# Up projection of five blocks by twenty block products per four row tiles, with chains begun from copies in PSUM

## The chip, the cores and the metric

The kernel runs on one core of a Trainium2 chip. The core has five engines with a queue each, and every engine works through its queue strictly in order: TensorE (PE, matrix products into PSUM), VectorE (DVE), ScalarE (ACT), GpSimd (POOL) and SyncE (SP, which here issues the DMAs). They wait for one another by semaphores. The metric is the device time of one execution in microseconds; of several executions the median is given.

## The reference

Two layers follow one another. The first is a linear attention with a state that decays per channel (4 sequences, 8 heads, 768 steps, 48 channels a head):

```python
for t in range(S):
    cur = einsum('bhd,bhe->bhde', u[None] * k[t], v[t])
    y[t] = einsum('bhd,bhde->bhe', r[t], state + cur)
    state = w[t][:, :, :, None] * state + einsum('bhd,bhe->bhde', k[t], v[t])
```

Its output, as 3072 tokens of 384 channels, goes through two projections with a gate in between:

```python
h = x @ w_in                        # (3072, 384) @ (384, 2048)
g = h * clip(h + 3.0, 0.0, 6.0) / 6.0
return g @ w_out                    # (3072, 2048) @ (2048, 384)
```

All of it is in fp32.

## The kernel before, in words

The 3072 tokens are 24 chunks of 128 (`L`), and four chunks make a block (`BC`), so there are six blocks, 0 to 5. The steps of attention of a chunk are two scans over its decays on VectorE (`back_scan` L372, `fore_scan` L381), scaling of r and k by them (`make_k`, `make_r`), a diagonal by eight small ScalarE operations (`diagonal` L431), scores and states on PE (`score` L440, `read_state` L514, `read_values` L523, `write` L536), and copies that put the result, transposed, into the block's `xT` (`leave` L606). Some channels take a way by DMA (`last_pair`, the steps `move`).

A block then is projected up and down. With 128 rows to a tile, the up projection has 16 row tiles of output (2048), 3 tiles of contraction (384, `NCC`) and 4 chunks as columns. The output stands transposed in two tiles `g0` and `g1`, one for each half of the block's 512 columns (`HB` = 256). The down projection takes one half at a time.

Block 0 is projected as written: three matmuls for each row tile and column group (`up` L639), then `clip` (L629) and `gate` (L650), and the first two chunks' `down` (L658) plain too. Blocks 1 to 5 use a fast block algorithm in which sums of blocks go into fewer products. Before the change it is a two-by-two scheme of Strassen's kind: for each of the eight pairs of row tiles (`q`), seven products over the first two tiles of contraction, with the third tile's four plain matmuls put into them, so 11 matmuls of 256 columns (`up_product` L740) in place of 12. The sums of weights are made once (`sum_in` L700), those of x once a block (`sum_x` L722, steps `tx`). Three banks of PSUM, `bankA`, `bankB` and `bankC`, hold a pair's sums. An intermediate value that two outputs need is read out of the bank and the next product added to the same bank after that. `up_read` does these reads, seven a pair: four copies on ScalarE (L749) and three adds on VectorE (L751). One of the copies (`u`) lies between products 6 and 7 of one bank. Each pair's outputs are then clipped (L629, ScalarE) and gated (L759, VectorE), 512 columns at a time.

The down projection of the half block, `p`, is likewise seven products of eight matmuls with 192 columns (`down_product` L791), in two parts of four matmuls, with sums on VectorE (`sum_g` L776, `sum_out` L712) and reads (`down_read` L804 and L806).

No engine's order is written out by hand. `Plan` holds each step with its engine, an assumed duration, what it comes after, a key (a due time in us, counted from the start of block 0's projection) and the rings of buffers that it holds until other steps have ended. Its `order` picks the step that could start earliest by the assumed durations, and of those that could start then the one with the smallest key; the steps are issued in that order, which fixes each queue. The assumed durations have no part in the running kernel apart from that order. `BASE` gives the blocks' due times, `START`, `CONV` and `UP` those of the first chunks, of the conversion of the weights from 64-bit floats (L340 to L359) and of block 0's up projection. Until the first up matmul (`up0.0.0`) the plan fills gaps on PE with products of an identity (`spin`, L1130).

The program for `sum` steps marks `port=True` for operations[...] and keeps them apart from each other.

The functions that the diff touches:

Of the kernel before, what the change touches and what calls it, by code (L numbers as in the profile page):

```python
# [27 lines left out]
LAG = 6.1  # L28
AHEAD = -3.5
LEAD = 2.5  # L30
BEHIND = (-1, -1, -1, 0, 6, 7)
BY_PE = 9
OWN = 0.07
SOLO = (0, 2, 3, 4, 5)
EARLY = 7
START = (-118.3, -135.2, -24.4, -60.3, -5.9, 13.2)
CONV = (-100.6, 7.2)
UP = (-68.7, 1.2, -9.3, 6.3)
SUMS = (52.1, 1.4)
LEAST = 2.0 ** -60  # L40

# [41 lines left out]
class Plan:  # L83
# [5 lines left out]
    HOP = 0.2  # L89
# [20 lines left out]
    def order(self):  # L110
# [13 lines left out]
        while open_:  # L124
            best = {}
            for n in open_:
# [4 lines left out]
                for a in after:  # L131
                    if steps[a][0] != engine:
                        t = max(t, end[a] + self.HOP)
                for r, _ in hold:
                    over = len(held[r]) - self.rings[r]
                    if over >= 0:
                        ends = sorted(max(end[a] + (self.HOP if steps[a][0] != engine else 0.0) for a in frees)
# [50 lines left out]
def fast_path(tc, feat, tok, wflat, ub, ug, moe_w_in, moe_w_out, out, flag, n_chunks):  # L188
# [21 lines left out]
    with ExitStack() as ctx:  # L210
# [34 lines left out]
        def constants():  # L245
# [16 lines left out]

            new_x(0)
# [99 lines left out]
        for r, k in (("E", 1), ("K", 2), ("W", 2), ("rk", 1), ("dg", 2), ("A", 2), ("kn", 1), ("S", 2), ("x", 2), ("kvs", 1), ("y", 1),  # L363
                     ("ps", 1), ("bankA", 2), ("bankB", 1), ("bankC", 2), ("clip", 2), ("g0", 1), ("g1", 1), ("o", 2),
# [68 lines left out]
        def score(i):  # L433
            d = st[i]
            d["a_ps"] = [pp.tile([128, P, HL], F32, name="bankB"), pp.tile([128, P, HL], F32, name="bankC", bufs=2)]
# [195 lines left out]
        def bank(name):  # L631
            return pp.tile([128, 512], F32, name=name, bufs=1 if name == "bankB" else 2)


        def up(f, c0, c1):
            b = blocks[0]
            h_ps = b["h", f, c0] = bank("bankA" if f % 2 else "bankC")
# [15 lines left out]
        def down(c, f0, f1):  # L653
            b = blocks[0]
            if f0 == 0:
                b["o", c] = bank("bankA")
# [23 lines left out]
        a_sums = {}  # L680
        b_sums = {}

        def a_slot(s, q):
            at = s * HF + q
            return a_sums[at // 6][:, at % 6 * 128:(at % 6 + 1) * 128]

        def sum_in(s, q):

            at = (s - 1 if s < 3 else 2) * HF + q
            if s != 3 and at // 6 not in a_sums:  # L690
                name = ("top", "more")[at // 6 % 2]
                a_sums[at // 6] = wk.tile([128, 6 * 128], F32, name=name)
            (a11, a21), (a12, a22) = ([w_in[:, q:q + 2, j, y, :] for y in range(2)] for j in range(2))
            def sums(k):
                at = k * HF + q
                return a_sums[at // 6][:, at % 6 * 128:(at % 6 + 2) * 128].rearrange("p (q j) -> p q j", q=2)
# [97 lines left out]
        def down_read(bk, p, what):  # L794
            b = blocks[bk]
            h = DM // 2
            if what == "s1":
                b["y", p] = wk.tile([L, 2, DM], F32, name="o")
# [671 lines left out]
```

## Time and profile before

| | us |
|---|---|
| median of 3 runs | 573.64 |
| the three runs | 573.64, 581.17, 572.21 |
| span of the profiled execution, first to last instruction | 570.5 |
| what lies between that span and the median; and the lowest run | 3.1; 1.7 |
| first matmul of block 0's up projection | 32.3 |
| first up matmul of blocks 1 to 5 | 151.8, 234.6, 320.6, 405.1, 489.0 |
| last matmul's end | 565.2 |

The profile gives no device time for the profiled execution itself, only its span; so the span stands beside the runs. The stretch before 32.3 us is attention for the first chunks with identity products in the gaps; then come block 0 (to 151.8) and five blocks. Attention for a later block is spread between the products of the one before. In the profile's groups "L740" is the line of the kernel, "bankA<-xT,w_in" the tile written and those read, "128x256" partitions by elements. An fp32 matmul of this kernel leaves two records, so 88 matmuls of an up projection are 176.

### The profile page before, as it was taken

To read this page: it belongs to the slowest core of one execution; us is meant where nothing else is said; L and a number is where in the kernel's file an instruction comes from. 1 tells how busy PE (TensorE), PEld (TensorE's weight loads), DVE (VectorE), ACT (ScalarE), POOL (GpSimd) and SP (SyncE) were. 2 spreads that over 40 slices of the span, in tenths; PEclk is the share of its full clock that TensorE was granted. 3 is DMA by queue.
4 is the path that set the end of the run, shared out by engine and by line. 5 is a ranking of instruction groups with operands and counts; after the bars stand their busy time and mean duration, and the time that the engine had idled before them with its cause. 6 is when DMAs were issued, how large, how long until landed. Compare 5 with 4: busy or idle time off the path is not lost.

```text
span 570.5 us, 13575 instructions
## 1 busy us (share of the span) xinstructions
PE 558.8 (98%) x5636; PEld 501.8 (88%) x5636; DVE 405.2 (71%) x713; ACT 273.5 (48%) x724; POOL 100.3 (18%) x111
## 2 busy tenths in 40 slices
PE   8999899999999999999999999999999999999996
PEld 8898587689888999988999988999988999988996
DVE  7989989988687858767879767879656625255350
ACT  4778664642565633276633366633266611355100
POOL 2000000245513321223123133123122000000000
PEclk9989899999999999999999999999999999999999
DMA  8977822531613236830368360366100001000001
GB/s 279 310 237 223 275 66 63 158 111 42 182 56 90 87 124 204 241 100 9 125 206 274 98 167 7 128 199 225 41 16 2 9 1 36 29 1 1 1 15 47
DMA packets 23078, 63.98 MB, mean 112 GB/s; under 512 B 3120, under 2 KB 10352, under 8 KB 23008
## 3 DMA queue, kind: packets, MB, share of 16 engines
q1 hardware_dynamic: 22880, 63.02, 36.0%
q8 instruction: 46, 0.75, 0.6%
q14 instruction: 24, 0.20, 0.1%
q10 hardware_dynamic: 128, 0.00, 0.0%
HBM read 57.31 MB, written 4.72 MB: 109 GB/s over the span
## 4 chain that ended last, share of the span: by engine, by line
PE 94%; DVE 2%; DMA 1%; ACT 1%; issue 1%; SPq 0%; DVEq 0%; ACTq 0%
PE bankA L791 20%; PE bankA L740 18%; PE bankC L791 10%; PE bankC L740 9%; PE bankB L740 6%; PE bankB L791 5%; PE bankC L639 3%; PE bankA L639 3%; PE bankA L658 3%; PE y_ps L514 3%; PE y_ps L523 2%; PE y_ps L536 2%; PE ps L456 2%; PE bankB L440 2%; DMA feat_in<-in_feat_dram 1%; PE bankA L1130 1%
## 5 line engine op out<-in xcount | busy, mean ns | idle before, releaser
L749 ACT COPY g<-bankA 128x256 f32<-128x256 f32 x120 | 44.3, 371 | 58.7 <-PE bankA L740 56.6
L791 PE MATMUL bankA<-w_out,g 128*128 128x192 f32 x352 | 63.9, 328 | 0.0
L629 ACT ACTIVATE clip<-g,three 128x512 f32<-128x512 f32 x80 | 57.9, 723 | 7.9 <-DVE g L751 7.2
L740 PE MATMUL bankA<-xT,w_in 128*128 128x256 f32 x240 | 60.2, 383 | 0.0
L791 PEld LDWEIGHTS bankA<-w_out,g 128*128 128x128 f32 x352 | 57.9, 190 | 0.9
L759 DVE SCALAR_TENSOR_TENSOR g<-clip,g 128x512 f32<-128x512 f32 x80 | 56.4, 707 | 2.8 <-ACT clip L629 2.6
L804 ACT ACTIVATE o<-bankA 128x192 f32<-128x192 f32 x33 | 10.9, 330 | 88.8 <-PE bankA L791 88.8
L740 PEld LDWEIGHTS bankA<-xT,w_in 128*128 128x128 f32 x240 | 44.8, 190 | 6.0
L431 ACT ACTIVATE A<-eyes,dg 128x64 f32<-128x64 f32 x192 | 49.2, 336 | 0.4
L606 ACT COPY xT<-y_ps 48x256 f32<-48x256 f32 x80 | 29.3, 366 | 37.3 <-PE y_ps L523 36.4
L392 POOL TENSOR_TENSOR K<-feat_in,E 112x512 f32<-112x512 f32 x17 | 21.5, 1266 | 136.6 <-PE bankC L440 121.6
L740 PE MATMUL bankB<-xT,w_in 128*128 128x256 f32 x160 | 41.1, 379 | 0.0
L751 DVE TENSOR_TENSOR g<-bankB,g 128x256 f32<-128x256 f32 x40 | 16.9, 423 | 32.4 <-PE bankB L740 30.7
L396 POOL TENSOR_TENSOR W<-feat_in,W 112x512 f32<-112x512 f32 x17 | 23.1, 1356 | 87.2 <-DVE W L381 87.2
L751 DVE TENSOR_TENSOR g<-bankC,g 128x256 f32<-128x256 f32 x40 | 16.8, 421 | 28.3 <-PE bankC L740 28.2
L740 PEld LDWEIGHTS bankB<-xT,w_in 128*128 128x128 f32 x160 | 30.4, 190 | 4.1
L381 DVE TENSOR_TENSOR_SCAN W<-feat_in,start 112x520 f32<-112x520 f32 x24 | 30.6, 1274 | 3.1 <-PE y_ps L514 3.0
L372 DVE TENSOR_TENSOR_SCAN E<-feat_in,back 112x520 f32<-112x520 f32 x24 | 30.0, 1250 | 2.5 <-DMA feat_in<-in_feat_dram 2.4
L791 PE MATMUL bankA<-bits,g 128*128 128x192 f32 x176 | 30.3, 328 | 0.4 <-DVE o L806 0.4
L791 PE MATMUL bankB<-w_out,g 128*128 128x192 f32 x176 | 30.4, 326 | 0.0
L791 PEld LDWEIGHTS bankA<-bits,g 128*128 128x128 f32 x176 | 28.8, 190 | 0.9 <-DVE o L806 0.7
L791 PEld LDWEIGHTS bankB<-w_out,g 128*128 128x128 f32 x176 | 28.9, 190 | 0.0
(277 smaller groups left out, 1213.8 us busy)
## 6 DMA issues: line engine op xcount, KB each, us to landing
feat_in<-in_feat_dram SPq DMA_DIRECT2D x23, 675.9 KB, 5.6
bits<-in_moe_w_in_dram SPq DMA_DIRECT2D x8, 768.0 KB, 9.6
bits<-in_moe_w_out_dram SPq DMA_DIRECT2D x8, 768.0 KB, 4.7
feat_in<-in_moe_w_in_dram SPq DMA_DIRECT2D x8, 768.0 KB, 4.3
feat_in<-in_moe_w_out_dram SPq DMA_DIRECT2D x8, 768.0 KB, 4.2
rk_in<-in_tok_dram SPq DMA_DIRECT2D x15, 384.0 KB, 5.9
v_in<-in_tok_dram SPq DMA_DIRECT2D x24, 192.0 KB, 4.0
out_dram<-o SPq DMA_DIRECT2D x24, 192.0 KB, 2.1
```

The costliest lines, as they stand in the source:

```text
L372: nc.vector.tensor_tensor_scan(out=E_[:, ::-1], data0=d["w"][:, :0:-1], data1=back.rearrange("q p t -> q (p t)")[:, ::-1], initial=0.0, op ...
L381: nc.vector.tensor_tensor_scan(out=W_, data0=d["w"][:, :-1], data1=starts[i % 2].rearrange("q p t -> q (p t)"), initial=0.0, op0=ALU.mult, ...
L396: early(i).tensor_mul(d["R"], d["r"], d["R"])
L431: nc.scalar.activation(out=d["A"][:, h, :], in_=eyes, func=ACT.Copy, scale=d["dg"][:, h])
L606: nc.scalar.copy(out=blocks[bk]["xT"][g * GP:g * GP + D, :, at:at + HL], in_=st[i]["y_ps"][(g ^ a) * GP:(g ^ a) * GP + D, a, :, :])
L629: nc.scalar.activation(out=c[:, :m], in_=src, func=ACT.Relu, bias=three, scale=1.0)
L639: nc.tensor.matmul(h_ps[:, :(c1 - c0) * L], lhsT=w_in[:, f // 2, j, f % 2, :], rhs=b["xT"][:, j, c0 * L:c1 * L], start=(j == 0), stop=(j = ...
L740: nc.tensor.matmul(b["p", q, to][:, :HB], lhsT=w, rhs=rhs, start=(n == 0 and k in (1, 2, 5)), stop=(n == len(terms) - 1 and k in (2, 3, 4) ...
L749: nc.scalar.copy(out=to, in_=src)
L751: nc.vector.tensor_add(to, src, to)
L759: nc.vector.scalar_tensor_tensor(out=g, in0=b["r", q, p], scalar=6.0, in1=g, op0=ALU.min, op1=ALU.mult)
L791: nc.tensor.matmul(b["d", p, to][:, :h], lhsT=a, rhs=w(), start=(f == 0 and k in (1, 2, 5)), stop=(f == HF - 1 and k in (2, 3, 4)), skip_g ...
```

## The change

The up projection of blocks 1 to 5 takes four row tiles together: four row tiles by three tiles of contraction by two column halves are 24 plain block products, and a scheme of 20 is used. There are two passes a block (`d`), each over two such groups (`z`), whose 256-column results lie side by side in one bank of 512. A product is then two matmuls, a pass 20 products, a block 80 matmuls. Instead of seven reads of 256 columns for each of eight pairs there are 19 of 512 columns for each of two passes: 8 on ScalarE and 11 on VectorE.

The sums of weights become 21 (`W_SUMS`), 128x512 each, once; nine of them write over `w_in` itself, after the last up product of block 0. The sums of x become 11 a block (`X_SUMS`), 128x256 each, in four steps.

Products are chained: `CHAINS` lists, for each bank, products (numbers) and reads (names) in the order that they must have. Some chains do not begin with an empty bank: ScalarE copies another chain's bank into the one bank `bankS` (reads `a4` and `a14`), and the next product adds to that. The down projection uses the same means: its read `s1` becomes a copy of bank A into `bankS`, product 2 adds to it and ScalarE reads `c11` out in one go; products 2 and 5 change places. The four bank names become one ring of four, `bank`, besides `bankS`. One product of zeros writes `bankS` at the start.

`WHEN` gives the due position of each of the 20 products in a pass; the last, 22, falls into the next pass. All due times are new, and so are the planner's assumed durations, the wait between engines among them (`HOP`). A parameter of the program for DMA scratch memory is set to 4096.

```diff
-LAG = 6.1
-AHEAD = -3.5
-LEAD = 2.5
+LAG = 8.196
+AHEAD = -4.96
+LEAD = -2.25
-START = (-118.3, -135.2, -24.4, -60.3, -5.9, 13.2)
-CONV = (-100.6, 7.2)
-UP = (-68.7, 1.2, -9.3, 6.3)
-SUMS = (52.1, 1.4)
+START = (-127.21, -154.12, -36.12, -115.85, 30.64, 32.42)
+CONV = (-75.91, 4.42)
+UP = (-75.43, 3.62, -8.89, 6.07)
+SUMS = (104.45, 0.18, 45.29)
+W_PLACE = ("e1", "e3", "e2", "w2", "w3", "w6", "e7", "w9", "e6", "w5", "w4", "w8", "e4", "w1", "w11", "e5", "w0", "w10", "e0", "w7")
+X_PLACE = ("w2", "e2", "e8", "e3", "w0", "e4", "w4", "w3", "w0", "e0", "e5", "w1", "w1", "w5", "e9", "w2", "e7", "w3", "e1", "e6")
+X_PARTS = (0, 4, 7, 9, 11)
+CHAINS = ((14, "a0", 19, "a1", 6, "a5", 0, "a10", 5, "a17"), (8, 15, "a2", 4, "a11"), (12, 17, "a3", 11, "a13"),
+          (1, "a4", 18, "a8"), ("a4", 3, "a6"), (9, "a9", 13, "a12", 2, "a14", 10, "a15"), ("a14", 7, "a16", 16, "a18"))
+READS = {"a0": (0, 0, None, 7), "a1": (0, 0, None, 6), "a3": (2, -1, 7, 7), "a4": (3, 1, None, "c4"),
+         "a5": (0, 0, None, 0), "a6": (4, 0, None, 4), "a7": (None, 1, 4, 6), "a2": (1, 1, 6, 6),
+         "a8": (3, 0, None, 1), "a9": (5, 0, None, 2), "a10": (0, 1, 4, 4), "a11": (1, 1, 2, 2),
+         "a12": (5, -1, 1, 3), "a13": (2, -1, 3, 3), "a14": (5, -1, None, "c6"), "a15": (5, -1, 0, 0),
+         "a16": (6, 1, 1, 1), "a18": (6, 1, 0, 5), "a17": (0, 1, 0, 0)}
+FINAL = ("a17", "a16", "a11", "a13", "a10", "a18", "a2", "a3")
+WHEN = (15, 0, 10, 4, 22, 18, 12, 13, 17, 1, 14, 11, 7, 5, 6, 19, 16, 8, 3, 9)
...
+        def sum_of(dst, a, b, sa, sb):
+            if sa < 0 and sb < 0:
+                nc.vector.scalar_tensor_tensor(out=dst, in0=a, scalar=-1.0, in1=b, op0=ALU.mult, op1=ALU.subtract)
+            elif sa < 0:
+                nc.vector.tensor_tensor(out=dst, in0=b, in1=a, op=ALU.subtract)
+            else:
+                nc.vector.tensor_tensor(out=dst, in0=a, in1=b, op=ALU.add if sb > 0 else ALU.subtract)
...
+        def sum_x(bk, part):
+            for dst, x, y, sx, sy in X_SUMS[X_PARTS[part]:X_PARTS[part + 1]]:
+                sum_of(x_at(bk, dst), x_at(bk, x), x_at(bk, y), sx, sy)
...
+        def up_product(bk, d, r):
             b = blocks[bk]
+            c, = (c for c, items in enumerate(CHAINS) if r in items)
+            fresh = CHAINS[c][0] == r
+            if fresh:
+                b["p", d, c] = bank()
+            last = [x for x in CHAINS[c] if isinstance(x, int)][-1] == r
+            for z in range(2):
+                nc.tensor.matmul(b["p", d, c][:, z * HB:(z + 1) * HB], lhsT=weight(W_PLACE[r])[:, 2 * z + d, :],
+                                 rhs=x_at(bk, X_PLACE[r]), start=fresh and z == 0, stop=last, skip_group_check=True)
+
+        def up_read(bk, d, name):
             b = blocks[bk]
+            c, sign, other, to = READS[name]
+            if isinstance(to, str):
+                b["p", d, int(to[1:])] = bank("bankS")
+                nc.scalar.activation(out=b["p", d, int(to[1:])], in_=b["p", d, c], func=ACT.Copy, scale=float(sign))
+                return
...
+            if sign == 0:
+                nc.scalar.copy(out=out_, in_=src)
             else:
+                nc.vector.tensor_tensor(out=out_, in0=src, in1=out_of(bk, d, other), op=ALU.add if sign > 0 else ALU.subtract)
...
             if what == "s1":
                 b["y", p] = wk.tile([L, 2, DM], F32, name="o")
+                b["d", p, "B"] = bank("bankS")
+                nc.scalar.copy(out=b["d", p, "B"][:, :h], in_=b["d", p, "A"][:, :h])
+                return
...
-                        (1, [], [("bankA", [r + "c21"])]), (2, [], [("bankB", [r + "c11"])]), (5, [], [("bankC", [r + "c12"])]),
+                        (1, [], [("bank", [r + "c21"])]), (5, [], [("bank", [r + "c12"])]), (2, [r + "s1"], []),
...
-    nc = _bacc.Bacc("TRN2", target_bir_lowering=False, num_devices=1)
+    nc = _bacc.Bacc("TRN2", target_bir_lowering=False, num_devices=1, dynamic_dma_scratch_size=4096)
```

## The prediction, made before the changed kernel was run

> **What bounds the kernel now.** I read the page's busy times and slices first, then the chain that ended last, then what TensorE waited for, then the stretches of single blocks, and last the instructions in order of time in one up projection. Busy times, slices and the chain's shares:
>
> ```profile
> PE 558.8 (98%) x5636; PEld 501.8 (88%) x5636; DVE 405.2 (71%) x713; ACT 273.5 (48%) x724; POOL 100.3 (18%) x111
> ...
> PE   8999899999999999999999999999999999999996
> ...
> DVE  7989989988687858767879767879656625255350
> ...
> PE 94%; DVE 2%; DMA 1%; ACT 1%; issue 1%; SPq 0%; DVEq 0%; ACTq 0%
> ```
>
> TensorE is busy in every slice and carries 94% of the chain. Busy matmul time overlaps itself, so the waits must agree. All that PE's matmuls waited for in the run (engine, line, who ended it: us in total, times, longest):
>
> ```profile
> PE y_ps L536 <- ACT kn L461: 1.6, 2, 0.9
> PE bankA L1130 <- POOL ident masks.py:199: 1.4, 1, 1.4
> PE y_ps L584 <- ACT xT L576: 0.6, 1, 0.6
> PE bankB L440 <- DVE A L447: 0.5, 1, 0.5
> PE bankA L791 <- DVE o L806: 0.4, 1, 0.4
> PE bankA L658 <- DVE w_out L359: 0.4, 1, 0.4
> ```
>
> They sum to 4.9 us, and the same view from 152 us on is empty: in blocks 1 to 5 no matmul waits. Stretches of one block each, and the last up projection (length; then PE, PEld, DVE, ACT, POOL busy):
>
> ```profile
> 120.00:151.80 31.80, 30.68 (x495) 28.00 (x485) 26.28 (x43) 12.78 (x41) 16.72 (x15) 1.00 0.33 98
> 151.80:234.50 82.70, 82.70 (x792) 76.01 (x793) 64.98 (x107) 40.88 (x113) 21.36 (x23) 1.00 0.41 124
> ...
> 320.40:405.80 85.40, 85.40 (x927) 78.22 (x926) 66.40 (x118) 42.02 (x116) 22.74 (x24) 1.00 0.45 138
> ```
>
> PE fills each block; VectorE takes 65 of some 84 us, ScalarE 42. A matmul taken out of an up projection is therefore worth its full issue time, as long as the work between matmuls keeps up. Groups that the change touches (last columns: busy, mean ns, idle before):
>
> ```profile
> L749 ACT COPY g<-bankA 128x256 f32<-128x256 f32 x120 | 44.3, 371 | 58.7 <-PE bankA L740 56.6
> L629 ACT ACTIVATE clip<-g,three 128x512 f32<-128x512 f32 x80 | 57.9, 723 | 7.9 <-DVE g L751 7.2
> L740 PE MATMUL bankA<-xT,w_in 128*128 128x256 f32 x240 | 60.2, 383 | 0.0
> L759 DVE SCALAR_TENSOR_TENSOR g<-clip,g 128x512 f32<-128x512 f32 x80 | 56.4, 707 | 2.8 <-ACT clip L629 2.6
> L751 DVE TENSOR_TENSOR g<-bankB,g 128x256 f32<-128x256 f32 x40 | 16.9, 423 | 32.4 <-PE bankB L740 30.7
> ```
>
> Price of a product, from the order of time in block 5: product 2 starts at 500.14 and product 7 at 501.00, two matmuls later.
>
> ```profile
> 500.14 1.03 PE L740 MATMUL bankB<-xT,w_in 128*128 128x256 f32 x4
> 500.34 0.37 ACT L749 COPY g<-bankC 128x256 f32<-128x256 f32 x1
> 500.61 0.72 ACT L629 ACTIVATE clip<-g,three 128x512 f32<-128x512 f32 x1
> 501.00 1.03 PE L740 MATMUL bankA<-T__5147,w_in 128*128 128x256 f32 x4
> 501.27 0.42 DVE L751 TENSOR_TENSOR g<-bankB,g 128x256 f32<-128x256 f32 x1 [1.23 <-PE bankB L740]
> ```
>
> That is 0.86 us for two, **0.431 us a matmul** (two records each); the chain says the same, 1.29 us for six records. The recorded end lies 0.17 us past the next issue (1.03 less 0.86), and VectorE's read starts 0.10 later.
>
> [...]423 (L751) and 686 (L776). I use 0.69 us for the new 512-wide reads. [...]x sums (L722, both in SBUF) take 0.41 us alone and 1.10 and 1.21 near 147 us with GpSimd active, while PSUM reads stay at 0.42. [...]
>
> **The change, part by part.**
>
> 1. *Fewer products.* Before: 8 pairs of tiles with 11 matmuls, 88 a block. After: 2 passes of 20 products with 2 matmuls, 80, all of 256 columns. Gone: 8 x 5 blocks = 40 matmuls x 0.431 = **17.2 us**. PE waited for nothing there, so all of it comes off the end unless new waits fill it.
>
> 2. *Waits inside chains.* 11 reads in a pass are followed by a product of the same or a seeded chain (a0, a1, a5, a10, a2, a3, a4, a9, a12, a14, a16): 110 waits, 50 on VectorE. By WHEN the next product comes at least two products later, 4 x 0.431 = 1.72 us. A VectorE read needs 0.17 + 0.10 + 0.69 + 0.04 (a copy on ScalarE ended at 150.17 and PE went on at 150.21) = 1.00 us: slack 0.72. A ScalarE read of 512: 371 ns at 256 plus [...]0.25 us (clip from PSUM 470 at 256, clip 723 at 512), 0.60; with its steps 0.85, slack 0.87. Before, product 6, its copy and product 7 stood only two matmuls apart, 0.86 us, of which 0.62 was needed, forty times, and PE didn't wait. A 512-wide operation just ahead costs the queue 0.60 us (gates start 0.60 apart), inside the slack; a scan costs some 1.15, which exceeds it by 0.4. Behind a late read wait on PE all later products, on its own engine the gates. Bounds: 0 (no gain: PE did not wait before), to 50 x 0.4 = 20 us if every VectorE read met a scan. A scan takes some 14% of VectorE's time in a stage, a pair of ready operations perhaps a fifth with 0.25 over: about 0.06 a read. I take **+3 us**.
>
> 3. *VectorE load.* Per block 22 reads of 0.69 for 24 of 0.42: +5.0; x sums 11 x 0.42 for 5: +2.6; the down projection's c11 goes to ScalarE: -0.7. 66.4 + 6.9 = 73.3 of 85.4 - 3.4 = 82.0 us, 89% as recorded, about 78% as queue time since records overlap (0.60 for 0.69). Still beneath PE. ScalarE: 16 x 0.60 for 32 x 0.37, -2.2 a block. Price nothing beyond part 2; the cover is 9 us of VectorE idle a block, and past it each us is PE time. The first product needs 4 of the 11 x sums, where it needed all 5.
>
> 4. *Weight sums.* 21 of 0.69 = 14.5 us for L700's 8.2 recorded: +6.3, all ahead of block 1's first product, the nine in place after block 0's last up. From 32.5 to 151.8 VectorE has 14 us idle (105.3 busy of 119.3), and chunks 8 to 10 can wait. Bounds 0 to 6.3, more if GpSimd contends; I take **+1**.
>
> 5. *Down projection.* Matmul count equal, 56 each half. s1 becomes a copy into PSUM that product 2 waits for; product 5 (2.6 us) now stands between, over the copy's 0.33. Nothing. At the end of a pass the last read, clip and gate (0.69 + 0.72 + 0.71, with steps 2.4 us) lie before down's second half; its first half, product 5's first half and the other row pair's product 1 (over 3.9 us) cover them. Nothing; uncovered, 1 us a block.
>
> 6. *Order and costs set anew, smaller DMA scratch.* All starts, keys and the planner's durations change, on the DMA queue too. PE spins 18.3 us on an identity before 32.5 us and waits 4.9 in all: it can win some of that or lose as much when VectorE, 88% busy from there to 151.8, serves another chunk first. Bounds -5 to +6; I take 0. [...]
>
> Sum: 570.5 - 17.2 + 3 + 1 = 557.3 us of span. The median shown lies 3.1 us above that span, the lowest run 1.7; with about 2, **559 us**.
>
> **Rivals.** *Reads late on VectorE* (B): 89% load in a queue kept in order speaks for it, the forty tighter waits met before against. At 0.2 us for each of 50 reads plus 2 for ScalarE's, stalls are 12, so 567. *Block 0 later* (C): the sums run into GpSimd's reads as L722 did, or the first up starts later; +7 beyond part 4: 566. *Slower than before* (D): VectorE's fixed order puts a gate ahead of an awaited read while the gate's clip is still behind eight-fold diagonal copies on ScalarE (1.06 us for four). PE then waits 1.06 + 0.72 + 0.60 - 0.72 = 1.7 us. Ten such events in 110 waits eat the gain; from 17 on it is over 2% slower; at 20, 590. Against it: such gates stood ahead of L751 reads too, and PE didn't wait. The products are counted from the code, so that fewer are issued is certain.
>
> **Numbers.** Forecast 0.65 (own range 552 to 563), B 0.15, C 0.13, D 0.07. The range 552 to 568 takes in the bounds of parts 4 and 6 and reaches B and C; D and half of B's upper part are left out. 2%, about what a measurement of this kernel can tell from no change, lies at 562.2: faster 0.70 (most of the forecast, the lower edges of B and C), same 0.23, slower 0.07.
>
> **What would show it.** Right: 800 records of up matmuls instead of 880, eight records per 1.72 us where PE runs on, block periods of 80 to 83 instead of 83 to 86 us, and at most 4 us of PE waits from block 1 on. Part 2 is wrong if PE waits on the bank reads by over 5 us; part 4 if block 1 begins after 153 us with PE waiting for weight sums; part 6 if the first up starts far from 32.5. What would make the whole wrong: a stall that recurs in every pass, since it counts tenfold.

## The result and the profile after

Four executions of each kernel: 574.21 us before, **565.75 us** after (medians; 564.42 to 566.59 after), a ratio of 0.987 with a 95% interval of 0.984 to 0.990. The ratio counts fast executions alone, without the one of 581.17 us before. The forecast was 559 us. The kernel is faster, by 8.5 us where the forecast, from 573.64, had 14.6, and does not reach the 2% (562.2 us) that the prediction set as its mark for "faster". The profiled execution took 565.76 us; its span is 563.6, against 570.5 before, so 6.9 us less.

The page of the changed kernel: busy times, slices of PE and VectorE, shares of the chain that ended last.

```profile
PE 542.6 (96%) x5530; PEld 482.8 (86%) x5530; DVE 451.6 (80%) x727; ACT 266.1 (47%) x655; POOL 105.8 (19%) x111
...
PE   8999999999999999999998999998999999999996
...
DVE  7989999999989978889997889997887836287440
...
PE 70%; DVE 24%; issue 3%; ACT 1%; DMA 1%; DVEq 0%; SPq 0%; ACTq 0%
```

PE is 16 us less busy, but VectorE, 2% of the chain before, now has 24%: somewhere PE waits for it. What PE's matmuls waited for from 140 us on (us in total, times, longest), a list that was empty before:

```profile
PE bank L788 <- DVE A L482: 2.9, 3, 1.1
PE bank L845 <- DVE A L482: 2.8, 2, 1.4
PE bank L788 <- DVE g L805: 2.1, 3, 1.0
PE bankS L845 <- ACT bankS L854: 0.8, 1, 0.8
PE bank L845 <- DVE o L863: 0.6, 1, 0.6
```

L788 is the up product, L845 the down product. Only 2.1 us are for reads inside chains (L805). Most is for `above` (L482), which masks attention's scores and frees their banks. The stretches of blocks 1 to 5 (length; then PE, PEld, DVE, ACT, POOL busy), and last that of block 4 before the change:

```profile
148.98:235.65 86.67, 84.86 (x962) 76.67 (x961) 73.19 (x109) 41.26 (x105) 29.30 (x29) 1.00 0.38 114
235.65:321.93 86.28, 83.25 (x902) 75.39 (x897) 76.92 (x119) 40.80 (x103) 26.04 (x24) 1.00 0.46 146
321.93:408.02 86.09, 83.24 (x901) 75.38 (x897) 76.58 (x119) 40.79 (x103) 24.52 (x24) 1.00 0.47 146
408.02:484.07 76.05, 74.94 (x649) 68.86 (x645) 49.94 (x93) 32.58 (x76) 5.08 (x6) 1.00 0.05 18
484.07:560.00 75.93, 74.10 (x404) 69.25 (x402) 36.01 (x60) 23.44 (x43) 0.00 (x0) 1.00 0.05 17
...
405.14:489.02 83.88, 83.66 (x794) 76.64 (x793) 42.34 (x88) 35.78 (x94) 6.66 (x7) 1.00 0.05 15
```

Blocks 1 to 3 last 86 to 87 us, no less than the 83 to 86 before; block 4 takes 76 instead of 84. These lengths can't be compared as they stand, because the new order has also moved attention: block 4 issues 649 matmul records where it had 794, and only 16 of the missing ones are its up projection's, while blocks 1 to 3 issue more than before. So the loss has to be counted by itself.

To see where PE's time went I took each matmul record's start to the next one's start and subtracted what such a record takes when nothing waits (216 ns at 256 columns, 162.8 at 192). What is left is "lost". In us, from the first up matmul on:

| | before | after |
|---|---|---|
| first up matmul of block 0 | 32.3 | 31.1 |
| block 0 up, lost | 1.1 | 5.1 |
| block 0 plain down, lost | 2.5 | 2.0 |
| up of blocks 1 to 5, without the lost part | 190.1 | 172.8 |
| the same, lost | 2.1 | 9.0 |
| down by seven products, lost | 4.3 | 8.5 |
| attention and the rest, whole | 70.2 | 67.1 |

So -17.3 by fewer products, +6.9 lost in up, +4.2 in down, +4.0 in block 0's up, -0.5 in its down, -3.0 and -1.2 in attention and at the start: -6.9 in all, the change of the span. By block, up and down together lose 1.1, 1.1, 1.2, 1.3 and 0.3 us in blocks 1 to 5 before, and 4.0, 5.1, 4.8, 1.8 and 0.4 after. The new loss sits in blocks 1 to 3, in which GpSimd is busy 25 to 29 us each; in block 4 it is busy 5 us.

Where such a loss starts shows in the order of time around a down projection in block 2 (start, duration, engine, line; in brackets idle time before and its releaser):

```profile
295.05 1.00 POOL L443 TENSOR_TENSOR rk<-rk_in 128x384 f32<-128x384 f32 x1
...
295.24 2.76 DVE L830 TENSOR_TENSOR S__3250<-g 128x512 f32<-128x512 f32 x2
...
296.13 1.33 POOL L444 TENSOR_TENSOR rk<-rk,u_bc 128x384 f32<-128x384 f32 x1
...
297.83 1.22 POOL L427 TENSOR_TENSOR K<-feat_in,E 112x512 f32<-112x512 f32 x1 [0.37 <-PE bank L475]
297.93 2.26 DVE L830 TENSOR_TENSOR g<-g 128x512 f32<-128x512 f32 x2
...
300.12 0.76 DVE L482 COPY_PREDICATED A<-mask,bank 128x256 f32<-128x256 uint8 x2
300.60 1.08 PE L845 MATMUL bank<-bits,S__3250 128*128 128x192 f32 x5 [1.42 <-DVE A L482]
```

Four S sums of 0.69 us take 5.0 us while GpSimd's three products run; `above` comes after them, and down product 5 waits 1.42 us. At the start of block 3 the same happens to the x sums:

```profile
321.87 0.42 DVE L736 SCALAR_TENSOR_TENSOR T__3556<-xT 128x256 f32<-128x256 f32 x1
322.33 1.29 DVE L740 TENSOR_TENSOR xT<-T__3556 128x256 f32<-128x256 f32 x1
323.54 0.87 DVE L738 TENSOR_TENSOR T__3556<-T__3556,xT 128x256 f32<-128x256 f32 x2
324.33 0.77 DVE L482 COPY_PREDICATED A<-mask,bank 128x256 f32<-128x256 uint8 x2
```

A sum of 0.42 us takes 1.29 beside K (GpSimd, 322.14 for 1.19 us), eleven sums stand ahead of `above`, and the up product that opens a chain begins only at 324.82. Adding up what VectorE's operations took beyond their usual time gives about 3 us for each of blocks 1 to 3 before the change, and about 7 after.

### The profile page after: what moved, and what is told of

Its sections match the earlier page's. It is cut to its first block, busy times and chain, and to the rows that moved or that the text cites. A ratio compares the mean times of both kernels' runs of the same rounds, so it can differ in the third digit from the quotient of the medians.

```text
span 563.6 us, 13312 instructions
## 1 busy us (share of the span) xinstructions
PE 542.6 (96%) x5530; PEld 482.8 (86%) x5530; DVE 451.6 (80%) x727; ACT 266.1 (47%) x655; POOL 105.8 (19%) x111
## 4 chain that ended last, share of the span: by engine, by line
PE 70%; DVE 24%; issue 3%; ACT 1%; DMA 1%; DVEq 0%; SPq 0%; ACTq 0%
PE bank L845 26%; PE bank L788 22%; PE bankS L845 5%; PE bankS L788 4%; PE bank L674 3%; PE bank L1204 2%; DVE g L805 2%; PE y_ps L549 2%; DVE E L407 2%; DVE A L482 1%; DVE g L813 1%; PE ps L491 1%; DVE w_out L394 1%; DMA feat_in<-in_wflat_dram 1%; PE y_ps L558 1%
## 5 line engine op out<-in xcount | busy, mean ns | idle before, releaser
L805 DVE TENSOR_TENSOR g<-bank,g 128x512 f32<-128x512 f32 x80 | 54.0, 683 | 15.8 <-PE bank L788 15.3
L845 PE MATMUL bank<-w_out,g 128*128 128x192 f32 x352 | 62.6, 328 | 0.0
L845 PEld LDWEIGHTS bank<-w_out,g 128*128 128x128 f32 x352 | 57.9, 190 | 0.8
L674 PE MATMUL bank<-xT,w_in 128*128 128x256 f32 x192 | 46.5, 395 | 0.0
L674 PEld LDWEIGHTS bank<-xT,w_in 128*128 128x128 f32 x192 | 37.4, 199 | 6.5 <-DVE g L685 0.4
L788 PE MATMUL bank<-xT,w_in 128*128 128x256 f32 x160 | 41.1, 381 | 1.1 <-DVE g L805 1.0
L803 ACT COPY g<-bank 128x512 f32<-128x512 f32 x50 | 29.0, 580 | 19.8 <-PE bank L788 19.5
L788 PEld LDWEIGHTS bank<-xT,w_in 128*128 128x128 f32 x160 | 29.9, 190 | 5.6 <-DVE g L805 1.9
L845 PE MATMUL bank<-more,g 128*128 128x192 f32 x176 | 30.7, 327 | 0.6 <-DVE o L863 0.6
L845 PE MATMUL bankS<-w_out,g 128*128 128x192 f32 x176 | 30.5, 327 | 0.8 <-ACT bankS L854 0.8
L788 PE MATMUL bank<-xT,bits 128*128 128x256 f32 x120 | 30.8, 379 | 0.0
L416 DVE TENSOR_TENSOR_SCAN W<-feat_in,start 112x520 f32<-112x520 f32 x24 | 29.5, 1230 | 0.3
L845 PEld LDWEIGHTS bankS<-w_out,g 128*128 128x128 f32 x176 | 28.8, 190 | 1.1 <-ACT bankS L854 1.1
L845 PEld LDWEIGHTS bank<-more,g 128*128 128x128 f32 x176 | 28.6, 190 | 1.0 <-DVE o L863 0.9
```

Source lines behind the costliest of these rows:

```text
L416: nc.vector.tensor_tensor_scan(out=W_, data0=d["w"][:, :-1], data1=starts[i % 2].rearrange("q p t -> q (p t)"), initial=0.0, op0=ALU.mult, ...
L674: nc.tensor.matmul(h_ps[:, :(c1 - c0) * L], lhsT=w_in[:, f // 2, j, f % 2, :], rhs=b["xT"][:, j, c0 * L:c1 * L], start=(j == 0), stop=(j = ...
L788: nc.tensor.matmul(b["p", d, c][:, z * HB:(z + 1) * HB], lhsT=weight(W_PLACE[r])[:, 2 * z + d, :], rhs=x_at(bk, X_PLACE[r]), start=fresh a ...
L803: nc.scalar.copy(out=out_, in_=src)
L805: nc.vector.tensor_tensor(out=out_, in0=src, in1=out_of(bk, d, other), op=ALU.add if sign > 0 else ALU.subtract)
L845: nc.tensor.matmul(b["d", p, to][:, :h], lhsT=a, rhs=w(), start=(f == 0 and k in (1, 5)), stop=(f == HF - 1 and k in (2, 3, 4)), skip_grou ...
```

## The experiments

My theory (A): the missing 6 us were lost because VectorE's sums of two SBUF tiles stand still behind GpSimd's products. Rivals: VectorE's load as such (B), the x sums' place ahead of `above` (C), the new order, the new form of the down projection, the clock at the start.

**GpSimd's products cut short.** K and R over 32 of 512 columns and rk over 32 of 384, from chunk 7 or 10 on, in the changed kernel and, as a control, in the one before; elsewhere the tiles keep older values. The main lines:

```diff
-            early(i).tensor_mul(d["K"], d["k"], d["E"][:, :, 1:])
+            m = HL if i < EARLY else 4
...
+            early(i).tensor_mul(d["K"][:, :, :m], d["k"][:, :, :m], d["E"][:, :, 1:1 + m])
...
-            early(i).tensor_mul(d["R"], d["r"], d["R"])
+            m = HL if i < EARLY else 4
+            early(i).tensor_mul(d["R"][:, :, :m], d["r"][:, :, :m], d["R"][:, :, :m])
...
-            nc.gpsimd.tensor_mul(d["rk"], d["rt"], d["kt"])
-            nc.gpsimd.tensor_mul(d["rk"], d["rk"], u_bc)
+            m = HD if i == BY_PE else 32
...
+            nc.gpsimd.tensor_mul(d["rk"][:, :m], d["rt"][:, :m], d["kt"][:, :m])
+            nc.gpsimd.tensor_mul(d["rk"][:, :m], d["rk"][:, :m], u_bc[:, :m])
```

> The changed kernel with GpSimd's products for K, R (from chunk 7 on) and rk (from chunk 10 on) cut to 4 of 64 columns per head half and 32 of 384; the rest of these tiles keeps older values, so this leaves out a part of the attention. The order of all queues is that of the changed kernel. In the changed kernel's trace the up and down matmuls lose 9.0 and 8.5 us between their starts beyond what their columns take (2.1 and 4.3 before the change), and VectorE's operations with two SBUF inputs are stretched by some 7 us in each of blocks 1 to 3. Theory A, GpSimd's reads stretch VectorE, and so scores and reads come late: the stretch goes, losses fall to about 4 and 5, span 556 to 558. Theory B, VectorE's queue is too long by itself: losses stay within 1.5 us, span 562 to 563.6.

> The same cut of GpSimd's products in the kernel before (control). There PE waits for nothing from block 1 on, so theory A and theory B both expect little: span 569 to 570.5. If it falls by over 3 us, the contention had a price before the change too, and it isn't the change that made it one.

Measured: 555.92 us (ratio to before 0.970, 0.965 to 0.976), lost 2.8 in up and 4.8 in down, nearly what the kernel before loses; the span, 550.1, falls further than A expected. The control: 574.39 (1.001, 0.999 to 1.003). So GpSimd's products cost the changed kernel 10 us and the kernel before nothing, though they stretched its sums too: there the stretch lay in slack. From 140 us on only these waits are left (the kernel has a few more lines):

```profile
PE bankS L848 <- ACT bankS L857: 0.8, 1, 0.8
PE bank L848 <- DVE o L866: 0.5, 1, 0.5
```

**Is it the reading, or GpSimd's being busy or late?** GpSimd writes constants into the same tiles instead (R, cut here, like K):

```diff
-            early(i).tensor_mul(d["K"], d["k"], d["E"][:, :, 1:])
+            if i < EARLY:
+                nc.vector.tensor_mul(d["K"], d["k"], d["E"][:, :, 1:])
+            else:
+                for _ in range(2):
+                    nc.gpsimd.memset(d["K"], 0.5)
...
-            nc.gpsimd.tensor_mul(d["rk"], d["rt"], d["kt"])
-            nc.gpsimd.tensor_mul(d["rk"], d["rk"], u_bc)
+            for _ in range(6):
+                nc.gpsimd.memset(d["rk"], 0.5)
```

> The changed kernel in which GpSimd's products K, R (chunks 7 to 23) and rk (chunks 9 to 23) are replaced by constants written into the same tiles, two such writes for K and for R, six for rk, so that GpSimd stays busy but reads nothing there; the products themselves are left out. VectorE's work and every engine's order stay as they are. If the price is that GpSimd and VectorE both read SBUF tiles: VectorE's sums keep their 0.69 us, TensorE's lost time falls to about 3 us (up) and 5 us (down), 553 to 559 us. If it is GpSimd's being busy, or being late with K, R and rk: VectorE's sums beside its writes are stretched all the same, 562 to 567 us.

Measured: **552.86 us** (0.965, 0.960 to 0.970), lost 3.4 and 4.8, with GpSimd busy 96.7 us. The same down projection as above, in its order of time (here the sums are L838):

```profile
287.87 2.79 POOL L452 MEMSET rk<- 128x384 f32 x6
...
288.43 1.28 DVE L838 TENSOR_TENSOR S__3306<-g 128x512 f32<-128x512 f32 x2
...
289.63 1.29 DVE L838 TENSOR_TENSOR g<-g 128x512 f32<-128x512 f32 x2
...
290.80 1.41 PE L853 MATMUL bank<-w_out,g 128*128 128x192 f32 x7
...
290.93 0.78 DVE L490 COPY_PREDICATED A<-mask,bank 128x256 f32<-128x256 uint8 x2
```

The four sums take 2.5 us beside 2.79 us of writes, and PE doesn't wait: product 5 of the down projection starts at 292.20 right behind the one shown. So in this kernel GpSimd's being busy cost nothing; what went away with its reads of SBUF is the 12.9 us between 565.75 and 552.86. These writes need no inputs, so GpSimd could also start earlier here. But lateness is not what costs: in the changed kernel, from 140 us on, no matmul waits for GpSimd, and VectorE waits for it 1.6 us in all.

**x sums of blocks 2 to 5 and gates of blocks 1 to 5 cut short**, each to 64 of 256 columns:

```diff
-                sum_of(x_at(bk, dst), x_at(bk, x), x_at(bk, y), sx, sy)
+                sum_of(x_at(bk, dst)[:, :m], x_at(bk, x)[:, :m], x_at(bk, y)[:, :m], sx, sy)
```
```diff
-            g = out_of(bk, d, u)
-            nc.vector.scalar_tensor_tensor(out=g, in0=blocks[bk]["r", d, u], scalar=6.0, in1=g, op0=ALU.min, op1=ALU.mult)
+            g = out_of(bk, d, u)[:, :, :64]
+            nc.vector.scalar_tensor_tensor(out=g, in0=blocks[bk]["r", d, u][:, :, :64], scalar=6.0, in1=g, op0=ALU.min, op1=ALU.mult)
```

> The changed kernel with the x sums of blocks 2 to 5 made over 64 of 256 columns (the rest of T keeps the values of block 1; this leaves out a part of the sums), order of all queues as it is. Theory C, the eleven x sums stand in front of the scores' masking (L482) on VectorE, which frees a bank for the third chain of a block: the three waits of 1.1 to 1.2 us at the start of blocks 2, 3 and 4 go, span 560 to 560.5. Theory A alone expects the same three waits to shrink by no more than the 0.86 us by which one x sum is stretched there: 561 to 561.5. Theory B expects 2 to 4 us, spread over the stage.

> The changed kernel with the gates of blocks 1 to 5 made over 64 of 256 columns of each row tile (the gate is left out elsewhere), order of all queues as it is. VectorE's load falls by some 0.4 us in each of 80 gates, 6.4 us a block, in the up stages alone. Theory B, the load itself: losses in the up projection fall from 9.0 to about 3, and the down's by what spills over, span 555 to 558. Theory A, contention: gates carry 1.4 us of some 7 us of stretch a block, so the up's losses fall by 1 to 3 us and the down's stay, span 560.5 to 562.5.

Measured: 562.74 us (0.981, 0.977 to 0.986) with short x sums; the waits of up products for `above` are gone, lost in up 5.0, in down still 8.4. So C is right for the starts of blocks, and for no more. With short gates 563.05 (0.981, 0.977 to 0.986): VectorE is 25 us less busy, and only 2.7 us are gained; the span, 560.5, is the lower end of what A gave. Its two longest waits:

```profile
PE bank L788 <- DVE A L482: 2.9, 3, 1.1
PE bank L845 <- DVE A L482: 2.4, 2, 1.2
```

They stand much as they did; the waits for reads inside chains fall from 2.1 to 0.6 us. Load has a share there, but B as the main cause falls.

**The products moved to VectorE, planner told.** rk first, then K, R and the decays:

```diff
-            nc.gpsimd.tensor_mul(d["rk"], d["rt"], d["kt"])
-            nc.gpsimd.tensor_mul(d["rk"], d["rk"], u_bc)
+            nc.vector.tensor_mul(d["rk"], d["rt"], d["kt"])
+            nc.vector.tensor_mul(d["rk"], d["rk"], u_bc)
...
-                plan.add(f"own{i}", "POOL", 2.05, do(own, i), [f"rkt{i}", "u"] + [f"own{i - 1}"] * (i > 0), k + 0.4,
+                plan.add(f"own{i}", "DVE", 1.04, do(own, i), [f"rkt{i}", "u"] + [f"own{i - 1}"] * (i > 0), k + 0.4,
```
```diff
-EARLY = 7
+EARLY = 24
```

> The changed kernel with the two rk products of chunks 9 to 23 (L443, L444) issued on VectorE, and told to the planner as VectorE's (1.04 us); the order is worked out anew from that. Same result, no work left out. GpSimd loses its 30 operations of 1.29 us; VectorE gains 30 of 128x384, some 0.5 us each, 15 us in all, about 3 us a block, against about 6.5 us a block by which its operations are stretched now. Theory A (what cost the gain is VectorE's SBUF sums standing still behind GpSimd's products): the waits of down product 5 behind stretched sums (1.58 us each at 300 and 386 us) and the waits for reads inside the chains go, those at the starts of blocks (x sums beside K) stay: 559 to 563 us. Theory B (VectorE's load itself is the price): more load, no gain or a loss, 566 to 570 us.

> The changed kernel with K, R and the decays of chunks 7 to 23 on VectorE too (EARLY 24), known to the planner; only rk stays on GpSimd. Same result, no work left out. GpSimd loses 34 operations of 1.3 us and 32 of 0.65 us, VectorE gains 34 of 0.68 us and 32 of about 0.35 us, 34 us in all, some 7 us a block: as much as the stretch takes now. Theory A: K no longer meets the x sums, so the waits at the starts of blocks shrink, those behind rk stay; with the load nearly the same: 560 to 566 us. Theory B: VectorE goes from 80% to over 83% and the waits grow: 567 to 573 us.

Measured: 571.22 us (0.997, 0.994 to 0.999) and 588.06 (1.028, 1.025 to 1.031). Both miss what either theory gave. With other durations the planner set the whole order differently, and PE waited for the x sums; the second kernel's first two waits:

```profile
PE bank L788 <- DVE T__1958 L736: 7.2, 1, 7.2
PE bank L788 <- DVE T__3629 L736: 3.6, 1, 3.6
```

These two say nothing of contention: the order moved with the edit. The next four keep it.

**The same, the planner told nothing.** Every queue stays as it was, apart from the operations that change engine: rk right ahead of the sum that reads it, then K too, then R too; and K alone.

```diff
-            d["rk"] = wk.tile([L, HD], F32, name="rk", bufs=1)
-            nc.gpsimd.tensor_mul(d["rk"], d["rt"], d["kt"])
-            nc.gpsimd.tensor_mul(d["rk"], d["rk"], u_bc)
...
         def own_sum(i):
...
+            d["rk"] = wk.tile([L, HD], F32, name="rk", bufs=1)
+            nc.vector.tensor_mul(d["rk"], d["rt"], d["kt"])
+            nc.vector.tensor_mul(d["rk"], d["rk"], u_bc)
             nc.vector.tensor_reduce(out=d["dg"].rearrange("s h o -> s (h o)"),
```
```diff
-            early(i).tensor_mul(d["K"], d["k"], d["E"][:, :, 1:])
+            nc.vector.tensor_mul(d["K"], d["k"], d["E"][:, :, 1:])
```
```diff
-            early(i).tensor_mul(d["R"], d["r"], d["R"])
+            nc.vector.tensor_mul(d["R"], d["r"], d["R"])
```

> The changed kernel with the two rk products of chunks 9 to 23 on VectorE, right ahead of the sum that reads them (L458), and the planner told nothing of it: every engine's order stays that of the changed kernel, but for the 30 operations that go from GpSimd to VectorE. Same result, no work left out. VectorE gains 30 of some 0.5 us (15 us, 3 us a block in blocks 1 to 3), GpSimd loses 38.7 us. Theory A (VectorE's sums of two SBUF tiles stand still behind GpSimd's products): the two waits of down product 5 (1.58 us each) and those behind the sums at 175, 268 and 355 us go, the block-start waits stay: 559 to 563 us. Theory B (load on VectorE is the price): 566 to 569 us.

> As the run before, with the products K of chunks 7 to 23 (L427) on VectorE too, 17 of 0.68 us, at their places in the order. Same result, no work left out. Theory A: the three waits at the starts of blocks, where K stretched the x sums, go as well; VectorE gains 26.5 us and loses some 18 of stretch: 556 to 561 us. Theory B: VectorE near 83% of the span, waits grow: 567 to 571 us.

> As the run before, with the products R (L431) on VectorE too, 17 of 0.69 us; GpSimd keeps the decays alone. Same result, no work left out. VectorE gains 38 us and loses some 21 of stretch. Theory A with nothing of B: 555 to 560 us. If VectorE's load begins to count here: 2 to 5 us above the run before.

> The changed kernel with K of chunks 7 to 23 alone on VectorE (17 of 0.68 us), rk and R left on GpSimd, every order unchanged. Same result, no work left out. By contention: the three waits at the starts of blocks (1.1 to 1.2 us each) go, the two of down product 5 stay: 562 to 564 us. If what K gained beside rk came from something else: 565 to 567 us.

Measured: rk 566.06 us (0.987, 0.981 to 0.993); rk and K **562.10** (0.980, 0.975 to 0.986); all three 563.35 (0.983, 0.977 to 0.989); K alone 562.89 (0.983, 0.978 to 0.989). Moving rk brings the loss in down from 8.5 to 5.7, as A said, but that in up from 9.0 to 10.3, so rk alone gains nothing. rk and K lose 8.4 and 5.3, K alone 6.8 and 6.1, and with K alone no up product waits for `above` any more. Of the ranges only the last was met: rk alone fell into B's, rk with K, at 562.1, lies between the two, and all three, 1.3 us above that, in neither range. A holds for the places it named, and part of the gain is given back.

**Is that VectorE's load?** rk and K on VectorE, and short gates as above:

> The kernel with rk and K on VectorE in unchanged order, and in it the gates of blocks 1 to 5 over 64 of 256 columns each (three quarters of the gates left out): VectorE has some 36 us less work. Against that kernel's 562.1 us: if VectorE's load is what holds the rest of the lost time (8.4 us up, 5.3 us down) now that the contention is gone, the waits for reads inside the chains go and it is 554 to 558 us; if it isn't load, 560 to 562 us. After the same cut the changed kernel itself gained 2.7 us.

Measured: 562.61 us (0.983, 0.979 to 0.988), no gain in the median; lost 7.3 in up, 5.1 in down. VectorE is busy 78% of the stretch from 149 to 484 us, hardly more than in the kernel with writes alone (77% of 149 to 480), which loses 3.4 and 4.8. So load as such does not explain the rest. The order of time in the kernel with rk and K on VectorE shows what stands ahead of an awaited read:

```profile
269.35 0.55 DVE L456 TENSOR_TENSOR rk<-rk_in 128x384 f32<-128x384 f32 x1
269.93 0.56 DVE L457 TENSOR_TENSOR rk<-rk,u_bc 128x384 f32<-128x384 f32 x1
270.52 0.55 DVE L458 TENSOR_REDUCE dg<-rk 128x8 f32<-128x384 f32 x1
270.99 0.68 DVE L805 TENSOR_TENSOR g<-bank,g 128x512 f32<-128x512 f32 x1
```

1.64 us of the diagonal's work (269.35 to 270.99) came ahead of the read in VectorE's queue, against a slack of 0.72 that the prediction gave such reads. With short gates three of the waits in up for such reads lie behind this group or a scan; that these are the whole remainder is not shown.

**GpSimd held back instead.** K on VectorE, and rk moved in GpSimd's order and made to wait for an S sum, the latest that the planner has at least 2.4 us ahead of rk's own sum:

```diff
+                if last > a:
+                    out.remove(f"own{i}")
+                    out.insert(last, f"own{i}")
...
-            early(i).tensor_mul(d["K"], d["k"], d["E"][:, :, 1:])
+            nc.vector.tensor_mul(d["K"], d["k"], d["E"][:, :, 1:])
...
+            if i in plan.behind:
+                bk, p, k, x = plan.behind[i]
+                m = HF // 2
+                seen_ = (blocks[bk]["g", p][:, HF + x * m, :1] if k == 3 else blocks[bk]["S", p][:, x * m, :1])
+                nc.gpsimd.tensor_copy(out=d["rk"][:, :1], in_=seen_)
             nc.gpsimd.tensor_mul(d["rk"], d["rt"], d["kt"])
```

> The kernel with K on VectorE, and rk on GpSimd held back: GpSimd first copies one column of the latest S sum (L830) that the planner has at least 2.4 us before the sum of rk, and so starts rk only after it; no VectorE work is added. Same result, no work left out. If contention at these sums is what is left, the waits of down product 5 and of the reads behind the sums go without new load: 557 to 561 us. If held-back rk comes late for its sum on VectorE (L458), VectorE's queue stands and it is 563 to 570 us. At 561 to 563 us it is worth nothing beside K on VectorE.

> The changed kernel itself once more, unaltered, to stand beside the variants on one chip: 564 to 567 us.

Measured: 571.38 us (0.996, 0.993 to 0.998), beside 566.24 (0.985, 0.980 to 0.990) for the changed kernel itself. That is above every range, and the trace shows that the edit did not do what it was for. In block 2 rk runs from 301.73 to 304.48 us, beside the last two of the four S sums, which take 2.89 us together from 302.13 on; block 3 has the same. VectorE waits for rk nowhere in these blocks, so it isn't late rk either. At the starts of blocks 2 to 4 up products wait 3.2 us for `above` again, though GpSimd stands idle there and each x sum takes its 0.42 us: eleven sums in a row, begun late, are enough. Down loses 10.1 us; what brings it so high is open, and the start of this profile was disturbed too (first up at 33.5, 4.2 us of waits for block 0's own `rk`). So nothing is shown of what holding GpSimd back would be worth.

The changed kernel's second profile, counted in the same way, loses 8.2 us in up and 8.5 in down, where the first had 9.0 and 8.5. Differences under 1 us in these losses mean little.

**More identity products ahead of the first up product:**

```diff
-    FILL = 0.75
+    FILL = 1.15
```

> The changed kernel with FILL 1.15 for 0.75: more identity products fill TensorE's idle time ahead of the first up product, nothing else is changed. In the trace of the changed kernel TensorE ran at half clock from 28.7 to 35.5 us, 4.4 us of it on products of block 0. If the clock comes up earlier with more filling, the half-clock time falls on the identity products and block 0 gains up to 2.2 us: 563.5 to 565.5 us. If the clock follows something else than the filling: 565.5 to 567 us, the half-clock window still beside block 0's first products.

Measured: 570.63 us (0.995, 0.993 to 0.997), outside both ranges. The profiled execution (567.92) began its first up matmul at 33.1 instead of 31.1, and a stretch at half the TensorE clock, 3.4 us long, still fell on it. So more filling did not help. That it delayed the start is not shown: the other variants, which fill alike, began anywhere from 29.5 to 33.5 us. The median lies 2.7 us above the profiled execution; that is open.

**The order's constants put back**, with the new products kept:

```diff
-LAG = 8.196
+LAG = 6.1
...
-START = (-127.21, -154.12, -36.12, -115.85, 30.64, 32.42)
-CONV = (-75.91, 4.42)
-UP = (-75.43, 3.62, -8.89, 6.07)
+START = (-118.3, -135.2, -24.4, -60.3, -5.9, 13.2)
+CONV = (-100.6, 7.2)
+UP = (-68.7, 1.2, -9.3, 6.3)
```

> The changed kernel with the eight constants of the order that the change set anew (LAG, AHEAD, LEAD, OWN, START, CONV, UP) put back to those before; the 20 products, their chains and the down projection stay new. Same result, no work left out. As the prediction had it (part 6 at nothing, bounds -5 to +6): within 6 us of the changed kernel, 560 to 572 us. If the new order holds the waits of the new form down: 570 to 580 us, with more waits for x sums and scores. If the new order itself brought the waits at the starts of blocks (scores standing in the ring of four banks): 558 to 563 us, and these waits gone.

Measured: 583.42 us (1.019, 1.011 to 1.026), above even the second range. Waits come back for x sums, for `s1` and for the final flag:

```profile
PE bankS L845 <- ACT bankS L854: 3.0, 5, 0.8
PE ps L918 <- DVE bad L914: 2.7, 1, 2.7
PE bank L845 <- DVE S__1623 L830: 2.3, 1, 2.3
PE bank L788 <- DVE T__2765 L736: 2.2, 1, 2.2
PE bank L788 <- DVE T__4494 L736: 2.1, 1, 2.1
```

Attention takes 82.2 us of PE instead of 67.1, down loses 13.3. With the old constants the new form is slower than the kernel before; the planner's assumed durations stayed new, so this is not the old order itself.

**The down projection's part undone:**

```diff
-            if k in (1, 5) and x == 0:
-                b["d", p, {1: "A", 5: "C"}[k]] = bank()
+            if k in (1, 2, 5) and x == 0:
+                b["d", p, {1: "A", 2: "B", 5: "C"}[k]] = bank("bankS") if k == 2 else bank()
...
-                b["d", p, "B"] = bank("bankS")
-                nc.scalar.copy(out=b["d", p, "B"][:, :h], in_=b["d", p, "A"][:, :h])
-                return
...
-                        (1, [], [("bank", [r + "c21"])]), (5, [], [("bank", [r + "c12"])]), (2, [r + "s1"], []),
+                        (1, [], [("bank", [r + "c21"])]), (2, [], [("bankS", [r + "c11"])]), (5, [], [("bank", [r + "c12"])]),
```

> The changed kernel with the down projection's part undone: product 2 begins on a fresh bank at once, s1 is ScalarE's scaled copy to o and c11 adds on VectorE, as before the change; the up projection stays new. As the prediction had it (part 5 at nothing): 565 to 567 us, with the 0.8 us wait for the s1 copy gone and c11's 22 additions back on VectorE. If the copy of the bank is the cause of the 4.2 us that the down products lost more than before: 561 to 563 us, and their lost time falls from 8.5 to about 4.5 us. If contention is the cause, that loss stays at 7.5 us or more.

Measured: 575.12 us (1.003, 1.001 to 1.006), down lost 9.3. This edit too let the planner reorder everything (a wait of 4.9 us for an x sum), so the time answers nothing about the down form. The kernels with GpSimd cut short do: with the new form in place down loses 4.8, against 4.3 in the kernel before and 4.0 in that kernel cut short alike, so the form itself costs 0.5 to 0.8. The kernel with the down part undone does not compute the same result. Its product 2 sets the start flag in `bankS`, where later chains begin with a copy; whether that is the cause is not shown.

## Why the prediction was wrong in size

1. **Fewer products, -17.2: right.** 880 records became 800, and without the lost part up went from 190.1 to 172.8 us: -17.3.

2. **Waits inside chains, +3: too low in sum, and mostly not the waits it priced.** Up lost 6.9 us more. Waits for in-chain reads are 2.1 us of the listed 5.0 in up; the other 2.9 lie at the starts of blocks, where a chain opens and the ring of four banks still holds scores. The step priced 110 waits within chains and none for opening one. Scores shared banks with up before the change too: there three names, `bankA`, `bankB` and `bankC`, had five buffers, and scores took one each of B and C, without a wait from 152 us on. What the single ring of four adds to these waits is not shown.

3. **VectorE load, "Price nothing beyond part 2": the step that failed.** It forecast 73.3 us of VectorE a block; blocks 2 and 3 had 76.6 to 76.9 (block 1 73.2). The difference is about the growth of the stretch, some 7 us a block in place of 3. The text had the mechanism at hand, sums at 1.10 and 1.21 instead of 0.41 us, and priced it for block 0 alone. "The cover is 9 us of VectorE idle a block" was the wrong cover: idle time later in a block doesn't help an `above` that stands behind stretched sums now. By the two runs that take most of GpSimd's reading away the contention is worth 10 to 13 us of the median. Without it the kernel takes 553 to 556 us, 3 to 6 below the forecast, so in sum the other terms were priced too high.

4. **Weight sums, +1: block 1 began at 148.98, earlier than the 151.72 before**, so "after 153" didn't come. But block 0's up lost 4.0 us more: 2.1 of them half clock on its first matmuls (28.7 to 35.5 us), 2.0 two waits at its end. They were hidden by a start 1.2 earlier and attention 3.0 shorter.

5. **Down projection, nothing: wrong by 4.2.** It counted the form, which costs under 1. Of the rest, 2.8 are the two waits of product 5 behind S sums stretched beside rk and K, operations that the change didn't touch but that now stood in each other's way; with rk alone moved away the loss falls by as much.

6. **Order, nothing: right in sum** (-1.2 and -3.0 against half clock and waits), but with the old constants the kernel takes 17.7 us more: they are a part of the change, not its trimming. That the smaller DMA scratch costs nothing was the author's assumption; no run takes it by itself.

With 2.1 us around the span for the 2 assumed, the sum missed the span by 6.3 us: +3.9 in part 2 and +4.2 in part 5, both for the most part the stretch that part 3 left out, and -1.7 in parts 4 and 6 together. PE's listed waits from block 1 on are 9.2 us, where at most 4 were to show the forecast right. Of the rivals, D, the slower case, did not come. C (566) gave the nearest time and named the right mechanism, "the sums run into GpSimd's reads", but placed it in block 0's weight sums, so its time is luck. B (567; by its own terms 568) came near by the wrong cause, since taking load away gained 2.7 us. "A stall that recurs in every pass" was named as what would make the whole wrong; here it recurs two or three times a block, eight times in all, from block 1 to the start of block 4.

## What to carry to other kernels

An empty list of waits says that there is slack, not how much. Where a change lengthens an in-order queue and shortens what covers it, price the stretch already in the trace at each place where someone waits next, even if it cost nothing before. And when a local edit goes through a planner, freeze the order first: three runs here measured the reordering, not the edit. Of the kernels tried that leave nothing out, rk and K on VectorE in unchanged order was the fastest (562.10 us, 0.980 against 0.987 and 0.985 for the change, intervals that overlap).

## What the runs showed of the hardware

Whether VectorE was held up went with where its operands lie and with what GpSimd did. In the changed kernel's trace the add of a PSUM bank and an SBUF tile takes 683 ns alone and 680 with GpSimd at work beside it, and the masked copy 433 and 438. The S sums of two SBUF tiles take 686 alone (62 of them) and 1125 in the mean beside GpSimd's products (26, from 641 to 1801), but 689 beside its writes (22, none over 693). A sum was held up for up to 1.1 us, with products of 1.2 to 1.5 us beside it. By the profile, whose GpSimd times are rough, it also went the other way: two S sums that began within 0.03 us of K's product (at 287.13 and 373.23 us) took 0.64 and 0.65 us, and that product took 1.71 us, where 1.18 is its shortest.

TensorE's half clock (0.50 granted from 28.7 to 35.5 us in the changed kernel's profile) came in lengths of 3.4, 6.8 and 10.2 us in the profiles (but for the end of the span, where it is cut off). All of them have one such stretch that begins between 26 and 39 us. Six have another in block 0 (the kernel before at 66.4; the changed kernel's second profile at 70.6, where its first has none), and only four kernels have one later than 140 us: those in which an edit let the planner order anew or put the old constants back. The one with K and R on VectorE, which waited up to 7.2 us for an x sum, has it at 151, 243 and 339 us (mean granted clock 0.970, against 0.992 in the changed kernel's). More filling did not keep the half clock off the first matmuls: 3.4 us of it still fell on them, where the changed kernel's profile has 6.8.

In the changed kernel's profile the 727 instructions of VectorE, 655 of ScalarE and 111 of GpSimd ran in the order in which the kernel issues them, none out of place; the same holds for 713, 724 and 111 before.
